# Row normalising and products with inverse sums given to GpSimd as well, in a two-layer attention and MLP kernel ordered by a planner

## The chip, the cores and the metric

The kernel runs on one core of one Trainium2 chip. The metric is device time in microseconds; the kernel before takes 855.15 us (median of 3 runs, 855.11 to 855.25). Five engines of the core work side by side, each through its own instructions in order: TensorE (PE in the profile), VectorE (DVE), ScalarE (ACT), GpSimd (POOL) and SyncE (SP, which issues the DMAs). They wait for each other by semaphores.

## The reference, cut

```python
def _layernorm(x, axis=-1, eps=1e-5):
    m = jnp.mean(x, axis=axis, keepdims=True)
    v = jnp.var(x, axis=axis, keepdims=True)
    return (x - m) / jnp.sqrt(v + eps)
...
    def _A_ref(x, wqkv, wo):                 # x: 1 x 2048 x 448, 16 heads of 28
        qkv = (x @ wqkv).reshape(B, S, 3, H, Dh).transpose(2, 0, 3, 1, 4)
        q, k, v = qkv[0], qkv[1], qkv[2]
        scores = jnp.einsum("bhqd,bhkd->bhqk", q, k) * Dh ** -0.5
        p = _softmax(scores, axis=-1)
        o = jnp.einsum("bhqk,bhkd->bhqd", p, v)
        return o.transpose(0, 2, 1, 3).reshape(B, S, D) @ wo
    def _B_ref(x, w1, b1, w2, b2):           # 448 -> 1792 -> 448
        h = jnp.einsum("bsd,df->bsf", x, w1) + b1
        r = jnp.where(h > 0, h, 0)
        return jnp.einsum("bsf,fd->bsd", r * r, w2) + b2

    x = A_x
    x = x + _A_ref(_layernorm(x), A_wqkv, A_wo)
    x = x + _B_ref(_layernorm(x), B_w1, B_b1, B_w2, B_b2)
    x = x + _A_ref(_layernorm(x), A_wqkv, A_wo)
    x = x + _B_ref(_layernorm(x), B_w1, B_b1, B_w2, B_b2)
    return x
```

## The kernel before

**The work.** Each of the two layers is an attention (A) and an MLP (B), with the same weights. Everything stays in the core's memory; `x_sb` holds the 2048 rows as 16 tiles of 128. Queries are worked on in blocks of 256 (two tiles; the last two of layer 2 are single tiles). The softmax numerators are the bulk: the scores of one head, 128 keys by 256 queries twice, make a *unit* of 128 x 512, and there are 2048 units in all.

**Groups of three.** `s_stream` (matmuls L892) writes three units into one score tile `sc` of 128 x 1536; there are two such tiles. `e_stream` (L917) turns them into `pt` by one exponential on ScalarE. 683 groups make up the run. `p_stream` (L1080) multiplies `pt` with `V_sb` on TensorE into `oT`, whose row 28 of each head holds the sum of the numerators.

**Units on DVE.** Where `apart` returns a unit, the third unit of a group is computed elsewhere and the exponential of that group has 1024 columns. Such a unit takes four steps: on DVE L973 (`take`: scores from PSUM into integers `v_i` or, for the third set of buffers, part of `K_sb`), on DVE L999 (`square`: a polynomial of the fraction, into `v_e`), on GpSimd L995 (`beside`: the power of two from the integer part) and on DVE L1017 (`close`: both multiplied into bf16, into `pt` or a tile of its own). `a_unit` issues the first, `a_rest` the others. `apart` refuses a unit if fewer than `STOP` units are left or fewer than `LEAD` groups have been made, if no set of buffers (two or three) is free, if keys or queries aren't there yet, if the planned load of DVE in the last `SPAN` us is over `BUSY` (`LOW` where the layers' work is behind its due line, `behind`, with `L0E` and `L0N` for layer 1), or if DVE's planned backlog with what such units still owe (`left`) is over `TB`.

**The other work** runs between: layer norms (`layernorm`: statistics L469 and L474 on DVE, variance and inverse root L496 and L497 on GpSimd, normalisation L579 on DVE into `xn`, transpose L519 on PE, copy L531 on DVE), Q, K and V (L634, L638, L666), and per query block a `chain`: output projection, residual L1216, layer norm, MLP with ReLU L1276 and square L1283, residual, and for layer 1 the norm and Q, K, V of layer 2. The first three blocks of layer 1 are `early`.

**Inverse sums.** For most query blocks `norm_pair` takes the sums of two groups of four heads out by DMA (`dn`), inverts them on DVE (L1188), spreads them over all rows by a way through DRAM (`scr`, `rec`), and multiplies `oT_sb` with `rec` into `oTn` (`mul`, L1207, 28 times). The last blocks use `norm_turn`, which does it by transposes on DVE (L1149 to L1165).

**The planner.** The order on each engine is made when the program is built. Every operation is an `Op` with engine, planned duration, operations it depends on and buffers it takes and frees. `Planner.run` picks the operation that can start first, and among equals the stream of the lowest priority number; `earliest` gives start and engine. An `Op` with `port=True` isn't planned on DVE while one is planned on GpSimd, and the other way round; on the chip nothing enforces it. In `earliest` before, the engine is the one that could start first:

```python
        if o.port:
            t = max(t, self.port["POOL" if o.eng[0] == "DVE" else "DVE"])
        ...
            if best is None or s < best[0] - 0.05:
                best = (s, e)
```

Before, L995 has `port=True` and 0.85 us (`EDUR`); L999, L1017, L1207 and L1283 have it on DVE; L579 hasn't. Priorities named in the change: `C_PRIO` for L973, `EPRIO` for L995, `V_WAIT` the time after which the rest of a unit becomes urgent. `NEAR` and `FAR` say how close to the next `p_stream` start a small or large matmul tile may still take a PSUM bank (`spare`); `KEEP` how long `p_stream` may wait for a unit from DVE.

**Filler.** TensorE also does matmuls whose result isn't used: `s_stream` repeats the score matmuls up to `MORE` times where the planned load is under `HOT` and there is room, and `heat` (L1334, `ident` by `xn`) adds one or two where the load is under `HEAT`.

Of the kernel before, what the change touches and what calls it, by code (L numbers as in the profile page):

```python
# [11 lines left out]
DT = mybir.dt  # L12
# [16 lines left out]
EXP_BASE = 91.0 * 2.0 ** 23 + 13573.0 * 2.0 ** 7  # L29
EXP_POLY = (4.803267716767392 * 2.0 ** 16, 14.031064225079138 * 2.0 ** 32)  # L30
OVER = 0.08
EDUR = 0.85
EPRIO = 1.5
EPOOL = 1
EMOD = 1
QUICK = 2
QUICK3 = 2
PRE = 0.5
# [4 lines left out]
DCLK = 0.2  # L43
OWN = 2
HALF = 320
L0E = 1310
L0N = 7.0
L1E = 1900
L1N = 5.6
# [12 lines left out]
AHEAD = (range(0, 4), range(0, 4), range(0, 4), range(0, 1))  # L62
SLACK = 0.5
WINDOW = 2.8
C_PRIO = 3.2
V_PRIO = 8.5
V_LATE = 4.0
V_LAST = 3
# [2 lines left out]
OWN3 = 0  # L71
FIRST = 50
V_FIRST = 9
V_WAIT = 3.5
NEAR = 4
FAR = 17
KEEP = 5
LAG = 12
LEAD = 20
LAST = 690  # L80
BUSY = 0.995
TB = 2.2
TB2 = 0.9
SPAN = 11
NPT = 11
NOS = 2
AEND = 0
HOT = 0.9
MORE = 3
HEAT = 0.76  # L90
HWIN = 3.4
NEAR_U = 0
LASTP = 3.2
# [4 lines left out]
THIRD = 1  # L98
NL = 0
NLP = 4.9  # L100
STOP = 100
HSTOP = 0
CHUNK = 2
EV = 2.9
# [24 lines left out]


class Op:
    __slots__ = ("eng", "dur", "fn", "deps", "acq", "rel", "mode", "sets", "start", "end", "res", "turn", "ready", "lat", "need", "got", "more", "room", "port")

    def __init__(self, eng, dur, fn, deps=(), acq=None, rel=None, mode="full", sets=(), lat=0.0, need=1, port=False):
        self.eng = eng if isinstance(eng, tuple) else (eng,)
        self.dur, self.fn, self.deps, self.mode, self.lat = dur, fn, deps, mode, lat
        self.rel = rel if isinstance(rel, list) else ([] if rel is None else [rel])
        self.acq = acq if isinstance(acq, tuple) or callable(acq) else (() if acq is None else (acq,))
        self.sets = sets if isinstance(sets, list) else ([sets] if sets else [])
        self.start = self.end = self.res = self.turn = None  # L140
        self.need, self.got, self.more, self.port = need, [], 0.0, port
# [5 lines left out]
class Planner:  # L147
# [22 lines left out]
    def earliest(self, o):  # L170
        t = 0.0
        for d in o.deps:
            if not isinstance(d, Op):
                d = self.tok.get(d)
            if d is None or d.end is None:
                return None, None
            same = d.eng[0] == o.eng[0] and len(o.eng) == 1
            t = max(t, d.end + d.lat + ((0.03 if same else 0.10) if d.eng[0] == "DVE" else
                                (0.0 if same and d.eng[0] != "DMA" else LAT[d.eng[0]])))
        acq = o.acq() if callable(o.acq) else o.acq  # L180
        if o.acq:
            free = [r.when() for r in acq if r.when() is not None]
            if not free:
                return None, None
            t = max(t, min(free))
        if o.port:
            t = max(t, self.port["POOL" if o.eng[0] == "DVE" else "DVE"])
        o.ready = t
        best = None
        for e in o.eng:  # L190
            s = max(t, self.clock[e])
            if e == "PE" and self.mode != o.mode:
                s = max(t, self.clock[e] + 0.1)
            if best is None or s < best[0] - 0.05:
                best = (s, e)
        return best

    def run(self):
        while self.streams:
            cands = []  # L200
            for st in self.streams:
                s, e = self.earliest(st[2]) if st[2] is not None else (None, None)
                if s is not None:
                    cands.append((s, st[0](s) if callable(st[0]) else st[0], e, st))
            assert cands, "no stream can go on"
            known = cands

            due = next((c[3][2].ready for c in cands if c[1] == 0), None)
            if due is None:
                due = next((c[0] + c[3][2].dur + LAT["ACT"] for c in cands if c[1] == 1), None)  # L210
            if due is not None:
                ok = [c for c in cands if c[2] != "PE" or c[1] == 0 or c[0] + c[3][2].dur <= due + self.slack()]
                cands = ok or cands
            s, _, e, st = min(cands, key=lambda c: (max(c[3][2].ready, self.clock[c[2]]) if c[2] == "PE" and self.turns() else c[0], c[1]))
            o = st[2]
            o.eng = (e,)
            if o.acq:
# [12 lines left out]
            if e == "PE":  # L230
                self.mode = o.mode
            if e in self.past:
                self.past[e] = [p for p in self.past[e] if p[1] > s - 40.0] + [(s, max(s, self.clock[e]))]
            for a in o.rel:
                a.got.append(o.end + o.lat + LAT[e])
                if len(a.got) == a.need:
                    a.res.rel[a.turn] = max(a.got)
            for key in o.sets:
                self.tok[key] = o
            st[2] = next(st[1], None)  # L240
            if st[2] is None:
                self.streams.remove(st)
# [3 lines left out]
def kernel(  # L246
# [12 lines left out]
    nc = tc.nc  # L259
# [220 lines left out]
    def layernorm(t0, nt, deps_of, early=False, mv=None, place=None, x_in=None, parts=False):  # L480
# [89 lines left out]
        for p0 in range(0, nt, wide):  # L570
            js = range(p0, min(p0 + wide, nt))
            own = Op("DVE", 0.0, None, acq=R_xn)
            yield own
            xs = []
            for j in js:
                xn = xns[2 * (own.turn % 2) + j % 2]

                def norm(e, j=j, xn=xn):
                    nc.vector.tensor_scalar(out=xn[:, 0:D], in0=x_sb[:, t0 + j, :],  # L579
                                            scalar1=mv[0][:, j, 0:1], scalar2=ln[j],  # L580
                                            op0=ALU.subtract, op1=ALU.mult)
                nm = Op("DVE", 0.39, norm, deps=[rss[j], *([] if x_in is None else [x_in])], sets=[("n", t0, j)] if early else ())
                yield nm
                xs.append((xn, nm))

            todo.append((p0, own, xs))
            if early and p0 + wide < nt:
                continue
            while todo:
                p0, own, xs = todo.pop(0)  # L590
                yield from turn(p0, own, xs)
# [370 lines left out]
    def a_unit(gi, x, src, unit, l):  # L962
# [20 lines left out]
    def a_rest(gi, c, box, unit):  # L983

        lin, low = EXP_POLY

        aside = unit[0] % EMOD < EPOOL

        def power(e):
            nc.vector.tensor_scalar(out=box["e"], in0=box["n"], scalar1=2.0 ** 22, scalar2=EXP_BASE,  # L990
                                    op0=ALU.mult, op1=ALU.add)

        def beside(e):
            box["h"], box["e"] = box["e"].bitcast(DT.float32), box["i"]
            nc.gpsimd.tensor_scalar(out=box["e"], in0=box["n"], scalar1=2.0 ** 22, scalar2=EXP_BASE,  # L995
                                    op0=ALU.mult, op1=ALU.add)

        def square(e):
            nc.vector.scalar_tensor_tensor(out=box["e"].bitcast(DT.float32) if aside else box["h"], in0=box["f"], scalar=lin, in1=box["f"],  # L999
                                           op0=ALU.add, op1=ALU.mult)  # L1000
        if aside:
            h = Op("DVE", 0.684, square, deps=[c], port=True)
            yield h
            left[0] -= 0.6
            p = Op("POOL", EDUR, beside, deps=[h], port=True)
            pl.spawn(EPRIO, iter([p]))
        else:
            p = Op("DVE", 0.42, power, deps=[c], port=True)
            yield p
            left[0] -= 0.34  # L1010
            h = Op("DVE", 0.684, square, deps=[c, p], port=True)
            yield h
            left[0] -= 0.6

        def close(e):
            pd = gbuf[gi]["pd"] = gbuf[gi]["pt"][:, 1024:1536] if gbuf[gi]["in"] else pd_of(o)
# [154 lines left out]
    def norm_pair(l, qb, g, pair):  # L1171
# [32 lines left out]
        yield r  # L1204

        def mul(e):
            nc.vector.tensor_tensor(out=oTn_of[l, qb][0][:, g:g + 2, 0:n], in0=both,  # L1207
                                    in1=box["r"][:, :, 0:n], op=ALU.mult)
# [176 lines left out]
```

## Time and profile before

The profiled execution took 857.11 us with its profile; its span, from the first instruction to the last, is 855.3 us. Of that, by engine:

| | busy us | share | what most of it is |
|---|---|---|---|
| PE | 813.1 | 95% | scores 306.9, `oT` from `pt` 153.0; ends of matmuls are modelled |
| ACT | 833.2 | 97% | exponentials L917, 821.4 |
| DVE | 780.0 | 91% | 231 units of three steps |
| POOL | 206.3 | 24% | L995, 164.4 |

A row of the groups reads: line, engine, operation, tile written and read, shapes, number, then busy time and mean duration of one in ns, then idle time before it and what ended it. A row of the timeline reads: start, duration, engine, line, operation, number. A row of the windows gives a stretch, its length, and for PE, weight loads, DVE, ACT and POOL the busy time and the number of instructions, then the granted clock of TensorE. A row of the waits gives who waited for whom, the sum, how often, and the longest.

The exponentials run from 12.3 to 840.6 us. POOL waits for L999 before L995 for 359.8 us in 122 times, which is time in which it has nothing to do.

### The profile page before, as it was taken

To read this page: it belongs to the slowest core of one execution; us is meant where nothing else is said; L and a number is where in the kernel's file an instruction comes from. 1 tells how busy PE (TensorE), PEld (TensorE's weight loads), DVE (VectorE), ACT (ScalarE), POOL (GpSimd) and SP (SyncE) were. 2 spreads that over 40 slices of the span, in tenths; PEclk is the share of its full clock that TensorE was granted. 3 is DMA by queue.
4 is the path that set the end of the run, shared out by engine and by line. 5 is a ranking of instruction groups with operands and counts; after the bars stand their busy time and mean duration, and the time that the engine had idled before them with its cause. 6 is when DMAs were issued, how large, how long until landed. Compare 5 with 4: busy or idle time off the path is not lost.

```text
span 855.3 us, 28520 instructions
## 1 busy us (share of the span) xinstructions
PE 813.1 (95%) x12287; PEld 434.4 (51%) x12287; DVE 780.0 (91%) x1510; ACT 833.2 (97%) x701; POOL 206.3 (24%) x326
## 2 busy tenths in 40 slices
PE   8999999999999999999999999999999999999998
PEld 4555555454545545455445544445544544545656
DVE  7999999999999999999898999999999999989744
ACT  7999999999999999999999999999999999999995
POOL 3211222222222222322222222321222123222100
PEclk9999999999999999999999999999999999999999
DMA  9200100000000000000000000011100000000000
GB/s 248 66 3 2 27 17 15 15 16 15 15 2 15 16 15 14 3 15 14 2 3 2 2 2 2 16 28 28 31 9 20 21 26 26 13 15 15 20 8 19
DMA packets 32315, 17.98 MB, mean 21 GB/s; under 512 B 17786, under 2 KB 31739, under 8 KB 32188
## 3 DMA queue, kind: packets, MB, share of 16 engines
q1 hardware_dynamic: 32188, 16.16, 6.9%
q8 instruction: 96, 1.57, 0.8%
q14 instruction: 31, 0.25, 0.1%
HBM read 13.87 MB, written 2.06 MB: 19 GB/s over the span
## 4 chain that ended last, share of the span: by engine, by line
ACT 41%; PE 32%; DVE 15%; issue 10%; DMA 1%; POOL 1%; ACTq 0%; SPq 0%; DVEq 0%
ACT pt L917 41%; PE mt L615 14%; PE sc L892 11%; PE oT L1080 5%; DVE v_i L973 2%; DVE v_e L999 2%; DVE pt L1017 1%; DVE r L1276 1%; DVE st L469 1%; DVE x_sb L1216 1%; PE sc L615 1%; PE mt L1334 1%; DVE xn L579 1%; DVE K_sb L999 1%; DVE K_sb L973 1%
## 5 line engine op out<-in xcount | busy, mean ns | idle before, releaser
L917 ACT ACTIVATE pt<-sc 128x1536 bf16<-128x1536 f32 (+1 forms) x683 | 821.4, 1403 | 7.6 <-PE sc L892 6.9
L892 PE MATMUL sc<-Q_sb,K_sb 32*128 32x256 bf16 (+1 forms) x5300 | 306.9, 266 | 29.7 <-ACT pt L917 22.2
L892 PEld LDWEIGHTS <-K_sb 32*128 32x128 bf16 x5300 | 135.3, 92 | 206.3 <-issue 155.6
L995 POOL TENSOR_SCALAR v_i<-v_i 128x512 int32<-128x512 int16 x166 | 118.1, 712 | 375.2 <-DVE v_e L999 359.8
L1080 PE MATMUL oT<-pt,V_sb 128*32 128x256 bf16 (+1 forms) x4056 | 153.0, 268 | 0.9 <-ACT pt L917 0.3
L615 PE MATMUL mt<-xnT,w 128*128 128x256 bf16 (+1 forms) x904 | 121.4, 270 | 0.4 <-DVE oTn L1165 0.2
L973 DVE TENSOR_SCALAR v_i<-sc 128x512 int32<-128x512 f32 x166 | 112.8, 680 | 8.0 <-PE sc L892 6.9
L1080 PEld LDWEIGHTS <-V_sb 128*32 128x32 bf16 x4352 | 90.9, 96 | 48.5 <-issue 45.3
L999 DVE SCALAR_TENSOR_TENSOR v_e<-v_i 128x512 f32<-128x512 uint16 x166 | 111.9, 681 | 0.3
L615 PEld LDWEIGHTS <-w 128*128 128x128 bf16 x952 | 77.1, 98 | 37.5 <-issue 29.5
L1276 DVE TENSOR_SCALAR r<-mt 128x512 bf16<-128x512 f32 x108 | 73.3, 679 | 8.4 <-PE mt L615 7.9
L995 POOL TENSOR_SCALAR K_sb<-K_sb 128x512 int32<-128x512 int16 x65 | 46.3, 712 | 141.0 <-DVE K_sb L999 130.4
L615 PE MATMUL mt<-w,V_sb 128*128 128x448 bf16 x274 | 67.6, 355 | 0.0
L1334 PE MATMUL mt<-xn,ident 128*128 128x448 bf16 x151 | 50.9, 356 | 1.4 <-DVE x_sb L1216 0.5
L1216 DVE TENSOR_TENSOR x_sb<-x_sb,mt 128x448 bf16<-128x448 bf16 x61 | 37.2, 610 | 14.4 <-PE mt L615 14.2
L973 DVE TENSOR_SCALAR K_sb<-sc 128x512 int32<-128x512 f32 x65 | 44.2, 681 | 4.6 <-PE sc L892 4.0
L999 DVE SCALAR_TENSOR_TENSOR K_sb<-K_sb 128x512 f32<-128x512 uint16 x65 | 45.0, 693 | 0.2
L1017 DVE SCALAR_TENSOR_TENSOR pt<-v_e,v_i 128x512 bf16<-128x512 f32 x62 | 42.0, 681 | 1.5 <-POOL v_i L995 1.5
L1017 DVE SCALAR_TENSOR_TENSOR V_sb<-v_e,v_i 128x512 bf16<-128x512 f32 x60 | 41.5, 694 | 1.9 <-POOL v_i L995 1.7
L496 POOL TENSOR_TENSOR ve<-mv,eps_t 128x2 f32<-128x2 f32 (+1 forms) x34 | 10.8, 318 | 118.1 <-DVE mv L474 117.9
L469 DVE BATCH_NORM_STATS2 st<-x_sb 128x6 f32<-128x448 bf16 x62 | 38.1, 615 | 0.9 <-DMA x_sb<-in_A_x_dram 0.7
L615 PEld LDWEIGHTS <-V_sb 128*128 128x128 bf16 x302 | 24.7, 98 | 25.0 <-issue 10.7
(105 smaller groups left out, 752.4 us busy)
## 6 DMA issues: line engine op xcount, KB each, us to landing
rec<-scr SPq DMA_DIRECT2D x54, 128.0 KB
x_sb<-in_A_x_dram SPq DMA_DIRECT2D x8, 224.0 KB
out_dram<-x_sb SPq DMA_DIRECT2D x15, 112.0 KB
w<-in_B_w_dram SPq DMA_DIRECT2D x1, 1568.0 KB
w<-in_B_w_dram SPq DMA_DIRECT2D x1, 1344.0 KB
dn<-oT_sb SPq DMA_DIRECT2D x54, 4.0 KB
V_sb<-in_A_wqkv_dram SPq DMA_DIRECT2D x4, 168.0 KB
scr<-dn SPq DMA_DIRECT2D x27, 8.0 KB
```

The source lines that it names most:

```text
L469: nc.vector.bn_stats(out=box["st"][:, :], in_=x_sb[:, t0 + j, :] if src is None else src())
L615: nc.tensor.matmul(box["t"][:, c0:c0 + n], lhsT=lhsT() if callable(lhsT) else lhsT, rhs=rhs, start=a, stop=b)
L892: nc.tensor.matmul(dst[k][:, i * nt * P:(i + 1) * nt * P], lhsT=K_sb[l][rows, g, (kb + i) * P:(kb + i + 1) * P], rhs=Q_sb[rows, g, t0 * P: ...
L917: t = nc.scalar.activation(out=pt[:, 0:n], in_=gbuf[gi]["sc"][:, 0:n], func=AF.Exp, scale=float(np.log(2.0)) * 2.0 ** -FRAC)
L973: t = nc.vector.tensor_scalar(out=box["i"], in0=two(src), scalar1=EXP_BIAS, scalar2=EXP_LOW, op0=ALU.add, op1=ALU.max)
L995: nc.gpsimd.tensor_scalar(out=box["e"], in0=box["n"], scalar1=2.0 ** 22, scalar2=EXP_BASE, op0=ALU.mult, op1=ALU.add)
L999: nc.vector.scalar_tensor_tensor(out=box["e"].bitcast(DT.float32) if aside else box["h"], in0=box["f"], scalar=lin, in1=box["f"], op0=ALU. ...
L1017: nc.vector.scalar_tensor_tensor(out=box["two"](pd), in0=box["h"], scalar=low, in1=box["e"].bitcast(DT.float32), op0=ALU.add, op1=ALU.mult)
L1080: nc.tensor.matmul(box["t"][DHP * hh:DHP * hh + DHP, 0:n], lhsT=V_sb[l][:, kb + i, 4 * g + hh, :], rhs=p[:, c0:c0 + n], start=begin and kb ...
L1216: nc.vector.tensor_tensor(out=x_sb[:, tb, lo:hi], in0=x_sb[:, tb, lo:hi], in1=t[:, 0:hi - lo], op=ALU.add)
L1276: nc.vector.tensor_scalar(out=r[:, 0:w], in0=t[:, 0:w], scalar1=0.0, scalar2=None, op0=ALU.max)
L1334: nc.tensor.matmul(t[:, 0:D], lhsT=ident[:, :], rhs=xns[0][:, 0:D], start=True, stop=True)
```

## The change

1. An operation may name several engines with a duration for each (`durs`). `earliest` now takes the engine on which it would end first, with `ASIDE` (2 us) added to DVE where GpSimd is the other.
2. The normalisation L579 may run on GpSimd (planned 0.6 us) or DVE (0.39), except in the `early` blocks, and has `port=True`. The product L1207 likewise (1.3 on GpSimd).
3. The power of L995 may run on either engine (`EDUR` 0.66 on GpSimd, 0.42 on DVE); a branch that put it on DVE for chosen units, which wasn't in use, is gone. Its order after the square stays.
4. Fourteen planning constants have new values.

```diff
-EDUR = 0.85
-EPRIO = 1.5
-EPOOL = 1
-EMOD = 1
+EDUR = 0.66
+EPRIO = 2.5
+ASIDE = 2.0
+XNP = 1
+XDUR = 0.6
+MULP = 1
+MDUR = 1.3
...
-L0E = 1310
+L0E = 1280
...
-C_PRIO = 3.2
+C_PRIO = 1.6
...
-V_WAIT = 3.5
-NEAR = 4
-FAR = 17
-KEEP = 5
+V_WAIT = 5
+NEAR = 6
+FAR = 9
+KEEP = 6
 LAG = 12
-LEAD = 20
+LEAD = 15
 LAST = 690
-BUSY = 0.995
+BUSY = 0.97
...
-SPAN = 11
+SPAN = 15
...
-MORE = 3
-HEAT = 0.76
+MORE = 1
+HEAT = 0.7
...
-STOP = 100
+STOP = 80
...
-        self.dur, self.fn, self.deps, self.mode, self.lat = dur, fn, deps, mode, lat
+        self.durs = dur if isinstance(dur, tuple) else (dur,) * len(self.eng)
+        self.dur, self.fn, self.deps, self.mode, self.lat = self.durs[0], fn, deps, mode, lat
...
-        if o.port:
-            t = max(t, self.port["POOL" if o.eng[0] == "DVE" else "DVE"])
         o.ready = t
         best = None
-        for e in o.eng:
+        for e, dur in zip(o.eng, o.durs):
             s = max(t, self.clock[e])
             if e == "PE" and self.mode != o.mode:
                 s = max(t, self.clock[e] + 0.1)
-            if best is None or s < best[0] - 0.05:
-                best = (s, e)
-        return best
+            if o.port:
+                s = max(s, self.port["POOL" if e == "DVE" else "DVE"])
+            late = s + (dur + ASIDE * (e == "DVE") if "POOL" in o.eng else 0.0)
+            if best is None or late < best[2] - 0.05:
+                best = (s, e, late)
+        return best[:2]
...
+            o.dur = o.durs[o.eng.index(e)]
             o.eng = (e,)
...
-                    nc.vector.tensor_scalar(out=xn[:, 0:D], in0=x_sb[:, t0 + j, :],
+                    (nc.vector if e == "DVE" else nc.gpsimd).tensor_scalar(out=xn[:, 0:D], in0=x_sb[:, t0 + j, :],
...
-                nm = Op("DVE", 0.39, norm, deps=[rss[j], *([] if x_in is None else [x_in])], sets=[("n", t0, j)] if early else ())
+                nm = Op(*((("POOL", "DVE"), (XDUR, 0.39)) if XNP and not early else ("DVE", 0.39)), norm, port=True, deps=[rss[j], *([] if x_in is None else [x_in])],
+                        sets=[("n", t0, j)] if early else ())
...
-        left[0] += 2.14 - 0.34 * (unit[0] % EMOD < EPOOL)
+        left[0] += 1.8
...
+        def square(e):
+            nc.vector.scalar_tensor_tensor(out=box["h"], in0=box["f"], scalar=lin, in1=box["f"],
+                                           op0=ALU.add, op1=ALU.mult)
+        h = Op("DVE", 0.684, square, deps=[c], port=True)
+        yield h
+        left[0] -= 0.6
...
+        def power(e):
+            (nc.vector if e == "DVE" else nc.gpsimd).tensor_scalar(out=box["e"], in0=box["n"], scalar1=2.0 ** 22, scalar2=EXP_BASE,
+                                                                   op0=ALU.mult, op1=ALU.add)
+        p = Op(("POOL", "DVE"), (EDUR, 0.42), power, deps=[h], port=True)
+        pl.spawn(EPRIO, iter([p]))
...
-            nc.vector.tensor_tensor(out=oTn_of[l, qb][0][:, g:g + 2, 0:n], in0=both,
-                                    in1=box["r"][:, :, 0:n], op=ALU.mult)
-        m = Op("DVE", 0.13 + 2 * n / 930, mul, deps=[r, oTn_of[l, qb][1]], rel=pair["own"], port=True)
+            (nc.vector if e == "DVE" else nc.gpsimd).tensor_tensor(out=oTn_of[l, qb][0][:, g:g + 2, 0:n], in0=both,
+                                                                   in1=box["r"][:, :, 0:n], op=ALU.mult)
+        m = Op(*((("POOL", "DVE"), (MDUR, 0.13 + 2 * n / 930)) if MULP else ("DVE", 0.13 + 2 * n / 930)), mul, deps=[r, oTn_of[l, qb][1]], rel=pair["own"], port=True)
```

More of the change, by code (lines that the diff above doesn't have):

```diff
@@ L131 @@
 class Op:
-    __slots__ = ("eng", "dur", "fn", "deps", "acq", "rel", "mode", "sets", "start", "end", "res", "turn", "ready", "lat", "need", "got", "more", "room", "port")
+    __slots__ = ("eng", "dur", "fn", "deps", "acq", "rel", "mode", "sets", "start", "end", "res", "turn", "ready", "lat", "need", "got", "more", "room", "port", "durs")
     def __init__(self, eng, dur, fn, deps=(), acq=None, rel=None, mode="full", sets=(), lat=0.0, need=1, port=False):
         self.eng = eng if isinstance(eng, tuple) else (eng,)
-        self.dur, self.fn, self.deps, self.mode, self.lat = dur, fn, deps, mode, lat
+        self.durs = dur if isinstance(dur, tuple) else (dur,) * len(self.eng)
+        self.dur, self.fn, self.deps, self.mode, self.lat = self.durs[0], fn, deps, mode, lat
         self.rel = rel if isinstance(rel, list) else ([] if rel is None else [rel])
@@ L578, in norm @@
                 def norm(e, j=j, xn=xn):
-                    nc.vector.tensor_scalar(out=xn[:, 0:D], in0=x_sb[:, t0 + j, :],
-                                            scalar1=mv[0][:, j, 0:1], scalar2=ln[j],
-                                            op0=ALU.subtract, op1=ALU.mult)
-                nm = Op("DVE", 0.39, norm, deps=[rss[j], *([] if x_in is None else [x_in])], sets=[("n", t0, j)] if early else ())
+                    (nc.vector if e == "DVE" else nc.gpsimd).tensor_scalar(out=xn[:, 0:D], in0=x_sb[:, t0 + j, :],
+                                                                           scalar1=mv[0][:, j, 0:1], scalar2=ln[j],
+                                                                           op0=ALU.subtract, op1=ALU.mult)
+                nm = Op(*((("POOL", "DVE"), (XDUR, 0.39)) if XNP and not early else ("DVE", 0.39)), norm, port=True, deps=[rss[j], *([] if x_in is None else [x_in])],
+                        sets=[("n", t0, j)] if early else ())
                 yield nm
@@ L985, in a_rest @@
         lin, low = EXP_POLY
-        aside = unit[0] % EMOD < EPOOL
-        def power(e):
[L990 to L1013, printed above, removed]
+        box["h"], box["e"] = box["e"].bitcast(DT.float32), box["i"]
+        def square(e):
[4 more added lines that the diff above has]
+        left[0] -= 0.6
+        def power(e):
+            (nc.vector if e == "DVE" else nc.gpsimd).tensor_scalar(out=box["e"], in0=box["n"], scalar1=2.0 ** 22, scalar2=EXP_BASE,
+                                                                   op0=ALU.mult, op1=ALU.add)
+        p = Op(("POOL", "DVE"), (EDUR, 0.42), power, deps=[h], port=True)
+        pl.spawn(EPRIO, iter([p]))
         def close(e):
```

## The prediction

> **What bounds the kernel now.** I read the first part of the page, then the chain, then what ScalarE (ACT) waited for.
>
> ```profile
> PE 813.1 (95%) x12287; PEld 434.4 (51%) x12287; DVE 780.0 (91%) x1510; ACT 833.2 (97%) x701; POOL 206.3 (24%) x326
> ...
> ACT 41%; PE 32%; DVE 15%; issue 10%; DMA 1%; POOL 1%; ACTq 0%; SPq 0%; DVEq 0%
> ```
> ```profile
> ACT pt L917 <- PE sc L892: 6.9, 14, 1.2
> ```
>
> ACT is busy 97% of the span, and its exponentials (L917) waited for scores 6.9 us in all. The trace puts the first exponential at 12.3 us and the end of the last at 840.6; before and behind them lie an opening and an end of about 27 us, which this change hardly touches. So the time is the work that ACT has between 12 and 841 us, and what counts is how many blocks of scores VectorE (DVE) takes off it. The groups by form give what one block is worth.
>
> ```profile
> L917 ACT ACTIVATE pt<-sc 128x1536 bf16<-128x1536 f32 x451 | 647.5, 1549 | 3.1 <-PE sc L892 2.4 <-ACT pt L917 0.5
> L917 ACT ACTIVATE pt<-sc 128x1024 bf16<-128x1024 f32 x232 | 253.0, 1121 | 4.6 <-PE sc L892 4.5
> ```
>
> 683 groups of three blocks; in 231 of them DVE takes the third, and the exponential has 1024 columns in place of 1536. The means differ by 0.428 us (neighbours overlap in time, but from end to end the medians of the trace are 1.343 and 0.917, so 0.426). **One more block on DVE shortens ACT's work by 0.43 us.** What it costs DVE, and what the change takes off DVE:
>
> ```profile
> L973 DVE TENSOR_SCALAR v_i<-sc 128x512 int32<-128x512 f32 x166 | 112.8, 680 | 8.0 <-PE sc L892 6.9
> L999 DVE SCALAR_TENSOR_TENSOR v_e<-v_i 128x512 f32<-128x512 uint16 x166 | 111.9, 681 | 0.3
> L1017 DVE SCALAR_TENSOR_TENSOR pt<-v_e,v_i 128x512 bf16<-128x512 f32 x62 | 42.0, 681 | 1.5 <-POOL v_i L995 1.5
> L579 DVE TENSOR_SCALAR xn<-x_sb,mv,rstd 128x448 bf16<-128x448 bf16 x64 | 30.6, 502 | 4.0 <-POOL rstd L497 4.0
> L1207 DVE TENSOR_TENSOR oTn<-oT_sb,rec 128x512 bf16<-128x512 f32 x27 | 18.3, 677 | 0.8 <-DMA rec<-scr 0.8
> ...
> L995 POOL TENSOR_SCALAR v_i<-v_i 128x512 int32<-128x512 int16 x166 | 118.1, 712 | 375.2 <-DVE v_e L999 359.8
> ```
>
> **What is taken off DVE.** Consecutive DVE instructions overlap: in the timeline below a step of 0.68 us begins at 401.66 and the next at 402.26, so one occupies the queue some 0.08 us less than its duration.
>
> ```profile
> 401.66 0.68 DVE L973 TENSOR_SCALAR v_i<-sc 128x512 int32<-128x512 f32 x1
> 402.26 0.69 DVE L579 TENSOR_SCALAR xn<-x_sb,mv,rstd 128x448 bf16<-128x448 bf16 x2
> ```
> ```profile
> 297.54 1.49 DVE L579 TENSOR_SCALAR xn<-x_sb,mv,rstd 128x448 bf16<-128x448 bf16 x2 [0.86 <-POOL rstd L497]
> ```
> ```profile
> 297.59 1.31 POOL L995 TENSOR_SCALAR v_i<-v_i 128x512 int32<-128x512 int16 x2
> ```
>
> Two normalisations take 0.69 us alone, but 1.49 beside two GpSimd powers: they hold each other up. That is why L579's mean is 0.502 and not 0.39, and L995's 0.712 and not 0.62 (its median).
> - Normalisations: 64, of which 6 (three opening blocks) stay. 30.6 - 6 x 0.39 = 28.3 us, less 58 x 0.08 of overlap: 23.7 us.
> - Products with inverse sums: 27 x 0.677 + 0.415 = 18.7, less 28 x 0.08: 16.5 us. The twelve products of L1165 stay.
> - Powers on DVE: the planner may now place them there, but charges 2 us for it; with GpSimd 24% busy I take none.
>
> Sum: 40.2 us of DVE time freed.
>
> **What it buys.** A block costs DVE 0.680 + 0.681 + 0.681 less 3 x 0.08 = 1.80 us. It also shortens the run by 0.43 us, in which DVE would have worked at the share that the long middle stretch shows:
>
> ```profile
> 100.00:800.00 700.00, 669.88 (x9975) 349.75 (x9970) 660.93 (x1244) 694.40 (x584) 180.15 (x274) 1.00 0.05 15
> ...
> 820.00:840.00 20.00, 18.41 (x473) 11.56 (x468) 6.38 (x18) 20.00 (x16) 0.00 (x0) 1.00 0.05 15
> ```
>
> The columns behind the length are PE, weight loads, DVE, ACT, POOL: DVE is busy 660.9 of 700 us (94%), ACT 99%. So 40.2 / (1.80 + 0.94 x 0.43) = 18.2 blocks.
> - STOP 100 to 80 and LEAD 20 to 15 open 20/3 + 5 = 11.7 more groups to DVE. DVE's steps run from 38.0 to 795.4 us; 19 exponentials start before and 34 after, so 231 of 630 groups, 0.37 each: 4.3 blocks. The last stretch has the room (6.4 of 20 us busy), the opening less: 3 blocks.
> - BUSY 0.97 over 15 us in place of 0.995 over 11: bites only where DVE would have been fuller than 97%, with the middle at 94%. Between 0 and 231 x 2.5% = 6 blocks lost; I take 1.5, because most stretches lie below it.
> - Ports: the planner no longer lets a normalisation or product on GpSimd run beside L999, L1017, L1283 on DVE. Between 0 and 6 blocks lost (next part but one); I take 1.
> - EDUR 0.66 in place of 0.85 agrees better with 0.62; C_PRIO, V_WAIT, NEAR, FAR, KEEP shift order. Each could gain or lose a few waits; ACT's scores waits are 6.9 us, so the gain is at most that, and a loss of the same size is my other bound. I take nothing.
>
> 18.2 + 3 - 1.5 - 1 = 18.7 blocks, x 0.43 = **8.0 us**.
>
> **What GpSimd takes on.** No row shows either operation there. A normalisation has one large input, like L995: 0.62 x 448/512 = 0.54 at the least, 0.99 (L995 held up) at the most; I take 0.57. A product has two inputs: at the least 0.62, at the most twice L995 held up, 2.0; if the inputs are read in turn, 1.24, and the diff charges 1.3: I take 1.27. 58 x 0.57 + 28 x 1.27 = 69 us on an engine with 649 idle. L995 should fall to 0.62-0.66, since its rival on the port is gone. Only one normalisation lies on the closing chain, L579 at 844.64 us (0.40): +0.2 us there. Queued behind a normalisation on GpSimd are powers, for which L1017 waits; behind it on PE, in order, stand its transpose and all scores after. The rival on queues prices that. No DMA is moved. A product keeps its `rec` and `oT_sb` tiles some 0.6 us longer, and SP's DMAs for the next pair wait for them, with the output stores queued behind; there are two of each, and L1207 comes every 10 us or more, so I take nothing (if a store were held, it would be by those 0.6 us).
>
> The Trainium skill (GPSIMD Engine Reference, 4.1 Engine selection) advises VectorE for elementwise work, GpSimd being about twice as slow with two inputs; its 3.1 gives about 2.6 cycles an element at 1.2 GHz, an estimate of 1.1 us and dispatch for a product. By that GpSimd's share changes by 5 us and the sum by nothing, for the engine has room.
>
> **The sum.** Span 855.3 - 8.0 + 0.2 = 847.5. The profiled run took 857.1, 1.8 around the span; the runs shown have a median of 855.15, 0.15 below the span. So **847.3 us**. Forecast band 844 to 850.
>
> **Rivals.**
> 1. *More than that* (13%): the DVE steps lose their hold-ups too (L1017 took 1.03 us at 103.10 beside a power), all 4.3 blocks come, and ACT's waits fall from 6.9 to 4: 25 blocks x 0.43 + 2.9 = 13.6, 841.5. For it: L999 and L1017 beside a power mostly take 0.68, so there is little to win there.
> 2. *The port eats the gain* (8%). L1017 at 103.10:
>
> ```profile
> 103.10 1.03 DVE L1017 SCALAR_TENSOR_TENSOR V_sb<-v_e,v_i 128x512 bf16<-128x512 f32 x1
> ```
>
> A power ran on GpSimd from 102.98, and the step took 0.35 us longer. If every added GpSimd microsecond that falls beside such steps (250 x 1.36 us and L1283's 46 in 847, 46%) were lost to DVE: 69 x 0.46 = 32 of the 40 us, 3.8 + 3 blocks, 2.9 us: 852.2. Against: of 69 L999 that overlap a power the mean is 0.698 against 0.679 for the others, and the plan keeps them apart. The Trainium skill (Advanced Engine Details and Errata, Mode Summary) states that such instructions of the two engines block each other; L579 at 297.54 agrees, those 69 mostly not.
> 3. *The freed time isn't used* (6%): the gates on DVE's load and backlog refuse the blocks. Only the 11.7 groups count, less BUSY's losses: 854.5, no change.
> 4. *Slower: PE waits for GpSimd* (11%). GpSimd works in order. A pair of normalisations there takes 2 x 0.57 against 0.69 (+0.45 us), and if a power stands in front, +0.62. The 29 transposes stand in PE's queue ahead of scores. PE has some 0.33 us of slack before ACT runs dry (it waited for ACT 68 times, 22.2 us). 29 x (1.07 - 0.33) = 21 us lost if all are hit; from 0.28 us for each transpose the 8 us are gone. Two in three hit: 861. For it: PE waited for L579 three times already, 2.0 us, up to 1.2. Against: the planner knows the longer duration, and L496 and L497 in front are on GpSimd anyway.
> 5. *Slower: TensorE's clock drops* (4%). MORE 1 and HEAT 0.7 take away filler: L1334's 151 matmuls and part of L892's repeats. The granted clock was 1.00 in every stretch from 20 us on. A slice at half clock lasted 3.4 us and would cost ACT about 1 us; one slice in twelve: +20, 867. Against: the longest gap between matmuls behind 20 us was 1.0 us.
>
> **Chances.** The forecast 58%. Faster by over 0.2% (1.7 us, about what a measurement here can tell from none): 58 + 13 + 8 = 79%; within: 6%; slower: 15%. The range that leaves out a fifth: 840.5 (below it lie ends of rival 1) to 858 (beyond it most of 4 and 5).
>
> **What would show it.** L917 with 1024 columns: about 250 of 683, ACT busy about 825; L579 on POOL x58 near 0.57, L1207 on POOL x28 near 1.27; L995 near 0.64; DVE still 90 to 92% busy. Wrong, if the count of 1024 stays near 231 (rival 3), if L999 and L1017 lengthen to 0.75 or more (2), if ACT's waits for L892 pass 12 us, with PE waiting for POOL (4), or if the clock shows slices below 1 (5).

## The result, and the profile after

The changed kernel takes 913.09 us (median of 4 runs, 910.37 to 914.63) beside 855.2 for the kernel before: ratio 1.067, 95% interval 1.064 to 1.070. The profiled execution took 910.37 us, its span is 908.1. Lines of the changed file are shifted by a few: L585 is the normalisation (L579 before), L1004 the power (L995), L924 the exponential (L917), L1201 the product (L1207), L525 the transpose (L519).

The first part of the page and its clock row, then the chain, of the changed kernel:

```profile
PE 824.1 (91%) x11998; PEld 427.8 (47%) x11998; DVE 764.5 (84%) x1441; ACT 836.4 (92%) x699; POOL 370.4 (41%) x417
...
PEclk9999989999999999999979999999999999989899
...
PE 38%; ACT 19%; DVE 19%; POOL 15%; issue 7%; DMA 0%; POOLq 0%; ACTq 0%; DVEq 0%
ACT pt L924 19%; PE mt L622 17%; PE sc L899 12%; POOL xn L585 11%; PE oT L1074 6%; DVE v_i L980 2%; DVE v_e L997 2%; DVE pt L1011 2%; DVE st L475 2%; PE mt L1328 2%; DVE x_sb L1210 2%; DVE r L1270 2%; POOL rstd L503 2%; POOL v_i L1004 1%; PE tp L525 1%
```

ACT fell from 97% of the span to 92% though its work grew by 3 us only: it stands still. GpSimd went from 206 to 370 us where 275 were forecast, and one of its lines, the normalisation, is now 11% of the chain. The clock row has slices below 9, which the one of before had not:

```profile
PEclk9999999999999999999999999999999999999999
```

The groups by form of the changed kernel (line, engine, operation, tiles, number, busy, mean ns, idle before):

```profile
L585 POOL TENSOR_SCALAR xn<-x_sb,mv,rstd 128x448 bf16<-128x448 bf16 x58 | 123.4, 2133 | 3.9 <-PE tp L525 0.7
L1004 POOL TENSOR_SCALAR v_i<-v_i 128x512 int32<-128x512 int16 x169 | 118.2, 699 | 278.5 <-DVE v_e L997 268.2 <-DVE oT_sb L1100 3.1 <-DVE mv L480 2.2
L1201 POOL TENSOR_TENSOR oTn<-oT_sb,rec 128x512 bf16<-128x512 f32 x27 | 36.7, 1359 | 15.0 <-DMA rec<-scr 13.8 <-PE sc L899 0.2
...
L924 ACT ACTIVATE pt<-sc 128x1536 bf16<-128x1536 f32 x446 | 638.1, 1518 | 35.2 <-PE sc L899 34.2 <-ACT pt L924 0.5
L924 ACT ACTIVATE pt<-sc 128x1024 bf16<-128x1024 f32 x237 | 252.8, 1095 | 21.5 <-PE sc L899 20.7 <-ACT pt L924 0.3
```

A normalisation takes **2.13 us** on GpSimd. The planner was told 0.6; on DVE it took 0.50. The product takes 1.36 where 1.3 was planned. And 237 of the exponentials have 1024 columns where it was 232: **five blocks more**, not nineteen. (One of them is the last group, which has only two blocks, so 236 come from DVE, and 231 before.) The waits of the changed kernel (who for whom, sum, how often, longest):

```profile
ACT pt L924 <- PE sc L899: 54.9, 50, 3.8
...
PEld L525 <- POOL xn L585: 42.5, 34, 2.4
PE tp L525 <- POOL xn L585: 35.2, 29, 2.3
```

ACT's wait for scores went from 6.9 to 54.9 us. The 48 us between them are nearly all of the 52.8 us by which the span grew. One such place in the timeline of the changed kernel, GpSimd, then TensorE, then ScalarE:

```profile
119.84 1.59 POOL L1201 TENSOR_TENSOR oTn<-oT_sb,rec 128x512 bf16<-128x512 f32 x1
121.42 4.07 POOL L585 TENSOR_SCALAR xn<-x_sb,mv,rstd 128x448 bf16<-128x448 bf16 x2
```
```profile
123.34 0.40 PE L525 MATMUL tp<-ident,xn 128*128 128x128 bf16 x4 [0.39 <-POOL xn L585]
125.54 0.61 PE L525 MATMUL tp<-ident,xn 128*128 128x128 bf16 x4 [1.81 <-POOL xn L585]
```
```profile
127.60 1.02 ACT L924 ACTIVATE pt<-sc 128x1024 bf16<-128x1024 f32 x1 [2.85 <-PE sc L899]
```

Two row tiles keep GpSimd for 4.07 us. PE has its transposes queued ahead of the next scores and stands 1.81 us before the second; ACT runs out and stands 2.85. Two windows around it, of the changed kernel (busy of PE, weight loads, DVE, ACT, POOL; then the clock, and the DMA's share and GB/s):

```profile
122.00:125.50 3.50, 0.91 (x11) 0.43 (x10) 1.75 (x3) 2.76 (x3) 3.49 (x2) 1.00 0.01 1
125.50:128.90 3.40, 3.36 (x27) 1.45 (x28) 2.05 (x5) 1.02 (x1) 0.62 (x1) 0.50 0.00 0
```

PE worked 0.91 of 3.5 us, and in the slice behind it the clock is half. The clock records show 13 such stretches between 20 us and the closing of the run, 61 us together; before, none.

### The profile page after: what moved, and what is told of

Same layout as the page of the kernel before. It is cut to its first block, busy times and chain, and to the rows that moved or that the text cites. A ratio compares the mean times of both kernels' runs of the same rounds, so it can differ in the third digit from the quotient of the medians.

```text
span 908.1 us, 28046 instructions
## 1 busy us (share of the span) xinstructions
PE 824.1 (91%) x11998; PEld 427.8 (47%) x11998; DVE 764.5 (84%) x1441; ACT 836.4 (92%) x699; POOL 370.4 (41%) x417
## 4 chain that ended last, share of the span: by engine, by line
PE 38%; ACT 19%; DVE 19%; POOL 15%; issue 7%; DMA 0%; POOLq 0%; ACTq 0%; DVEq 0%
ACT pt L924 19%; PE mt L622 17%; PE sc L899 12%; POOL xn L585 11%; PE oT L1074 6%; DVE v_i L980 2%; DVE v_e L997 2%; DVE pt L1011 2%; DVE st L475 2%; PE mt L1328 2%; DVE x_sb L1210 2%; DVE r L1270 2%; POOL rstd L503 2%; POOL v_i L1004 1%; PE tp L525 1%
## 5 line engine op out<-in xcount | busy, mean ns | idle before, releaser
L924 ACT ACTIVATE pt<-sc 128x1536 bf16<-128x1536 f32 (+1 forms) x683 | 825.5, 1371 | 56.7 <-PE sc L899 54.9
L1004 POOL TENSOR_SCALAR v_i<-v_i 128x512 int32<-128x512 int16 x169 | 118.2, 699 | 278.5 <-DVE v_e L997 268.2
L899 PEld LDWEIGHTS <-K_sb 32*128 32x128 bf16 x5058 | 127.7, 93 | 220.2 <-issue 171.8
L1074 PE MATMUL oT<-pt,V_sb 128*32 128x256 bf16 (+1 forms) x4058 | 156.3, 272 | 1.1 <-DVE pt L1011 0.7
L980 DVE TENSOR_SCALAR v_i<-sc 128x512 int32<-128x512 f32 x169 | 115.6, 685 | 21.2 <-PE sc L899 20.5
L585 POOL TENSOR_SCALAR xn<-x_sb,mv,rstd 128x448 bf16<-128x448 bf16 x58 | 123.4, 2133 | 3.9 <-PE tp L525 0.7
L997 DVE SCALAR_TENSOR_TENSOR v_e<-v_i 128x512 f32<-128x512 uint16 x169 | 116.3, 695 | 0.4
L1004 POOL TENSOR_SCALAR K_sb<-K_sb 128x512 int32<-128x512 int16 x67 | 48.2, 719 | 136.8 <-DVE K_sb L997 119.2
L525 PE MATMUL tp<-ident,xn 128*128 128x128 bf16 x252 | 24.4, 228 | 36.1 <-POOL xn L585 35.2
L1011 DVE SCALAR_TENSOR_TENSOR pt<-v_e,v_i 128x512 bf16<-128x512 f32 x69 | 47.1, 685 | 3.8 <-POOL v_i L1004 3.8
L1201 POOL TENSOR_TENSOR oTn<-oT_sb,rec 128x512 bf16<-128x512 f32 (+1 forms) x28 | 37.4, 1336 | 21.4 <-DMA rec<-scr 20.2
L1328 PE MATMUL mt<-xn,ident 128*128 128x448 bf16 x104 | 38.5, 392 | 6.1 <-POOL xn L585 6.0
```

What stands on the lines that cost most here:

```text
L585: (nc.vector if e == "DVE" else nc.gpsimd).tensor_scalar(out=xn[:, 0:D], in0=x_sb[:, t0 + j, :], scalar1=mv[0][:, j, 0:1], scalar2=ln[j], ...
L899: nc.tensor.matmul(dst[k][:, i * nt * P:(i + 1) * nt * P], lhsT=K_sb[l][rows, g, (kb + i) * P:(kb + i + 1) * P], rhs=Q_sb[rows, g, t0 * P: ...
L924: t = nc.scalar.activation(out=pt[:, 0:n], in_=gbuf[gi]["sc"][:, 0:n], func=AF.Exp, scale=float(np.log(2.0)) * 2.0 ** -FRAC)
L980: t = nc.vector.tensor_scalar(out=box["i"], in0=two(src), scalar1=EXP_BIAS, scalar2=EXP_LOW, op0=ALU.add, op1=ALU.max)
L997: nc.vector.scalar_tensor_tensor(out=box["h"], in0=box["f"], scalar=lin, in1=box["f"], op0=ALU.add, op1=ALU.mult)
L1004: (nc.vector if e == "DVE" else nc.gpsimd).tensor_scalar(out=box["e"], in0=box["n"], scalar1=2.0 ** 22, scalar2=EXP_BASE, op0=ALU.mult, op ...
```

## The experiments

All but the two measurements of forms were timed beside the kernel before, whose median was 855.3 to 855.6. In each diff the minus line is the changed kernel (or the kernel before, where said).

**e1: normalisations back on DVE.**

```diff
-XNP = 1
+XNP = 0
```

> The changed kernel with the 58 normalisations back on DVE (XNP 0); products, powers and all constants as changed. Theory D (a normalisation takes 2.13 us on GpSimd instead of the 0.57 assumed, so transposes in PE's queue wait, ACT runs dry and the clock falls behind that): nearly all of the 58 us comes back, 850 to 860 us, granted clock 0.99 or more, ACT waits for scores under 15 us. Rival F (the smaller filler, MORE 1 and HEAT 0.7, lets the clock fall by itself): the clock stays near 0.97 and the time above 885. Rival M (products on GpSimd): time above 885, with PE waiting for L1201.

860.45 us (ratio 1.005, 1.004 to 1.007), clock 0.998, ACT's wait for scores 10.3 us. As theory D has it; rivals F and M fall as causes of the loss: filler and products are as changed here, and 53 of the 58 us are gone.

```profile
ACT pt L924 <- PE sc L899: 10.3, 10, 3.2
```

**e2: filler as before.**

```diff
-MORE = 1
-HEAT = 0.7
+MORE = 3
+HEAT = 0.76
```

> The changed kernel with MORE 3 and HEAT 0.76 as before; normalisations stay on GpSimd. Theory D: the waits for the normalisation stay (PE on xn 60 us or more in all), the filler can't be issued while PE's queue stands still, so the clock stays below 0.98 and the time above 895. Rival F: clock 0.99 or more and the time below 880.

916.99 us (ratio 1.073, 1.070 to 1.076), clock 0.968. More filler doesn't hold the clock while PE's queue stands: theory D.

**e3: the kernel before with the normalisations on GpSimd, nothing else.**

```diff
-                    nc.vector.tensor_scalar(out=xn[:, 0:D], in0=x_sb[:, t0 + j, :],
+                    (nc.gpsimd if e == "POOL" else nc.vector).tensor_scalar(out=xn[:, 0:D], in0=x_sb[:, t0 + j, :],
...
-                nm = Op("DVE", 0.39, norm, deps=[rss[j], *([] if x_in is None else [x_in])], sets=[("n", t0, j)] if early else ())
+                nm = Op("DVE" if early else "POOL", 0.39 if early else 0.6, norm, port=not early, deps=[rss[j], *([] if x_in is None else [x_in])], sets=[("n", t0, j)] if early else ())
```

> The kernel before with one edit: the 58 normalisations on GpSimd, planned at 0.6 us; constants, filler, products as before. Theory D: it takes most of the loss by itself, 895 to 925 us, with the normalisation at about 2.1 us on GpSimd and the clock below 0.98. Rivals F and M: no filler or product has changed, so 845 to 865.

920.55 us (ratio 1.074, 1.070 to 1.078), clock 0.975 in the profiled execution. This single edit makes the whole loss: 65 us here, 58 with the other changes.

```profile
L579 POOL TENSOR_SCALAR xn<-x_sb,mv,rstd 128x448 bf16<-128x448 bf16 x58 | 124.2, 2145 | 6.8 <-PE mt L1334 3.1 <-PE tp L519 0.5
```

**e4 and e5: what GpSimd takes for which form.** Behind the last row tile of the kernel before, three instructions of each form, alone on the core.

```diff
+    for k in range(3):
+        nc.gpsimd.tensor_scalar(out=xns[0][:, 0:D], in0=x_sb[:, NTB - 1, :], scalar1=rs[:, 0:1], scalar2=rs[:, 1:2], op0=ALU.subtract, op1=ALU.mult)
+    for k in range(3):
+        nc.gpsimd.tensor_scalar(out=xns[1][:, 0:D], in0=x_sb[:, NTB - 1, :], scalar1=0.5, scalar2=0.25, op0=ALU.subtract, op1=ALU.mult)
...
```

> The kernel before with 18 instructions added on GpSimd behind its last row tile, three of each form, alone on the core (its time means nothing): 128x448 bf16 to bf16 with two per-row scalars, with two constants, with one per-row scalar; 128x448 to f32 with two per-row scalars; to bf16 with one per-row scalar and one constant; 128x224 to f32 with two per-row scalars. Theory P (the per-row scalars make it slow): about 1.87 us with two, 0.55 with two constants, between them with one. Rival B (bf16 in or out makes it slow): 1.87 with constants too, and less with f32 out. Rival H (held up by DVE in the kernel): all about 0.57 when alone.

Groups of e4: L1359 two per-row scalars, L1365 the same to f32, L1361 two constants, L1363 a multiplication alone, L1369 half the columns:

```profile
L1359 POOL TENSOR_SCALAR xn<-x_sb,mhalf 128x448 bf16<-128x448 bf16 x3 | 5.6, 1860 | 8.5 <-DVE x_sb L1216 8.3
L1365 POOL TENSOR_SCALAR v_e<-x_sb,mhalf 128x448 f32<-128x448 bf16 x3 | 5.6, 1858 | 0.2
...
L1361 POOL TENSOR_SCALAR xn<-x_sb 128x448 bf16<-128x448 bf16 x3 | 5.1, 1708 | 0.2
L1363 POOL TENSOR_SCALAR xn<-x_sb,mhalf 128x448 bf16<-128x448 bf16 x3 | 4.2, 1403 | 0.2
L1369 POOL TENSOR_SCALAR v_e<-x_sb,mhalf 128x224 f32<-128x224 bf16 x3 | 3.3, 1108 | 0.2
```

None of the three theories: it is slow alone (against H), slow with constants (against P), and with f32 out it takes 1.86 too (against B, as far as the output goes). Between it and the power at 0.62 stood the types and the pair of operations. So e5 crossed them.

> As e4, 18 instructions behind the last row tile on GpSimd, three of each (its time means nothing). e4 had subtract-then-multiply slow (1.71 us) even with two constants, while the kernel's power (multiply-then-add with constants, 128x512 int16 to int32) takes 0.62. Theory O (the pair of operations decides): multiply-then-add takes 0.55 to 0.65 on 128x448 bf16, with constants and with two per-row scalars; subtract-then-multiply and add-then-multiply take 1.7 us or more, on int16 to int32 too. Rival T (the types decide: bf16 is slow, int16 is not): multiply-then-add on bf16 takes about 1.7 too, and subtract-then-multiply on int16 to int32 about 0.6.

Groups of e5: L1362 and L1366 subtract then multiply; L1358, L1360, L1364 multiply then add; L1368 add then multiply; constants in L1360, L1364 and L1366:

```profile
L1362 POOL TENSOR_SCALAR xn<-x_sb,mhalf 128x448 bf16<-128x448 bf16 x3 | 5.6, 1860 | 0.2
L1366 POOL TENSOR_SCALAR v_e<-v_i 128x448 int32<-128x448 int16 x3 | 5.1, 1709 | 0.2
L1358 POOL TENSOR_SCALAR xn<-x_sb,mhalf 128x448 bf16<-128x448 bf16 x3 | 2.1, 715 | 8.5 <-DVE x_sb L1216 8.3
L1368 POOL TENSOR_SCALAR xn<-x_sb,mhalf 128x448 bf16<-128x448 bf16 x3 | 2.1, 713 | 0.3
L1364 POOL TENSOR_SCALAR v_e<-v_i 128x448 int32<-128x448 int16 x3 | 1.7, 565 | 0.2
L1360 POOL TENSOR_SCALAR xn<-x_sb 128x448 bf16<-128x448 bf16 x3 | 1.7, 564 | 0.2
```

**The pair of operations decides**, not the types: multiply-then-add is 0.56 with constants on either type, subtract-then-multiply 1.71 on either. Per-row scalars add 0.15. Theory O was wrong in one point: add-then-multiply is fast as well (0.71), so in a pair it is the subtraction in front that is slow. That is not the whole rule: e4's multiplication alone, with no subtraction, took 1.40. What the fast forms have in common was not tried further.

**e6: the planner is told the true duration.**

```diff
-XDUR = 0.6
+XDUR = 1.9
```

> The changed kernel with one number: the planner is told 1.9 us for a normalisation on GpSimd instead of 0.6. It still stays there. Theory Q (most of the 58 us comes from the wrong number: PE's queue has the transposes, and all behind them, before the rows are ready): PE's waits for the normalisation fall below 15 us, the clock is back at 0.99 or more, 865 to 880 us. Rival L (the slow instruction itself costs it, through GpSimd's queue and the port it shares): above 895 us with the clock below 0.98.

874.09 us (ratio 1.020, 1.018 to 1.023), clock 0.992. Waits for the normalisation in e6:

```profile
ACT pt L924 <- PE sc L899: 16.2, 19, 2.5
...
PE mt L1328 <- POOL xn L585: 5.2, 4, 1.5
...
PEld L525 <- POOL xn L585: 0.9, 4, 0.3
```

The instruction is as slow as before (1.99 us), but PE finds its rows ready. So 39 us of the loss came from the order that the wrong number made, though the units on DVE fell to 222 (from 236).

**e9: the normalisation as add-then-multiply.** GpSimd makes the negative means behind the inverse roots, 0.29 us for two tiles.

```diff
-XDUR = 0.6
+XDUR = 0.72
...
                 nc.gpsimd.tensor_tensor(out=rstd[:, a:b], in0=ve[:, a:b], in1=mhalf[:, a:b], op=ALU.pow)
+                if not early:
+                    nc.gpsimd.tensor_scalar(out=rstd[:, a + 2:b + 2], in0=mv[0][:, a:b, 0], scalar1=-1.0, scalar2=None, op0=ALU.mult)
+                    for j in range(a, b):
+                        negs[j] = rstd[:, j + 2:j + 3]
-            rs = Op("POOL", 0.95, rsqrt, deps=[mv[1][b - 1]], sets=[("rs", t0 + a)] if early else ())
+            rs = Op("POOL", 0.95 if early else 1.2, rsqrt, deps=[mv[1][b - 1]], sets=[("rs", t0 + a)] if early else ())
...
-                                                                           scalar1=mv[0][:, j, 0:1], scalar2=ln[j],
-                                                                           op0=ALU.subtract, op1=ALU.mult)
+                                                                           scalar1=negs[j], scalar2=ln[j],
+                                                                           op0=ALU.add, op1=ALU.mult)
```

> The changed kernel with the normalisation written as add-then-multiply: GpSimd also makes the negative mean of two row tiles (one small instruction behind the inverse root), and a normalisation there is (x + negative mean) x inverse root, which e5 measured at 0.71 us; the planner is told 0.72, and 1.2 in place of 0.95 for the inverse root. Products stay on GpSimd, constants as changed. Theory O (the operation pair was the trouble): normalisation 0.7 to 0.8 us, clock 0.99 or more, 855 to 864 us, and no faster than before, since e1, e7 and e8 show that the products on GpSimd cost 5 to 7 us and freed DVE time hardly becomes blocks. Rival L (normalising rows on GpSimd costs the time through its queue, whatever the duration): 875 or more.

863.34 us (ratio 1.009, 1.008 to 1.011), clock 0.996. In e9:

```profile
L593 POOL TENSOR_SCALAR xn<-x_sb,rstd 128x448 bf16<-128x448 bf16 x58 | 50.8, 881 | 3.5 <-POOL rstd L505 0.2
```

0.88 us in the kernel, somewhat over the 0.7 to 0.8 expected, and 50 us of the loss are gone. This run changes the instruction and the number together; by e6 the number alone is worth 39 of the 50. Rival L falls. But it is still slower than before, with DVE at 753 us instead of 780: the freed time is idle.

**e7: products on DVE too.**

```diff
-XNP = 1
+XNP = 0
...
-MULP = 1
+MULP = 0
```

> The changed kernel with normalisations and products on DVE: what is left is the constants and the planner's choice for the power. e1 (normalisations on DVE, products on GpSimd) took 860.4. If the products on GpSimd are the cause of e1's 5 us over before: 853 to 856. If the constants are: 859 to 862.

856.07 us (ratio 1.000, 0.999 to 1.001). The constants and the free choice for the power together neither gain nor lose (no power went to DVE); the products on GpSimd cost the 4.4 us between e7 and e1. All five blocks came with them: DVE takes 231 in e7, 236 in e1, and 236 again where the normalisations move too.

**e8: the kernel before with the products on GpSimd, nothing else.**

```diff
-            nc.vector.tensor_tensor(out=oTn_of[l, qb][0][:, g:g + 2, 0:n], in0=both,
+            nc.gpsimd.tensor_tensor(out=oTn_of[l, qb][0][:, g:g + 2, 0:n], in0=both,
...
-        m = Op("DVE", 0.13 + 2 * n / 930, mul, deps=[r, oTn_of[l, qb][1]], rel=pair["own"], port=True)
+        m = Op("POOL", 1.3, mul, deps=[r, oTn_of[l, qb][1]], rel=pair["own"], port=True)
```

> The kernel before with one edit: the 28 products on GpSimd, planned at 1.3 us (measured 1.34). By the prediction's sum for this part (16.5 us of DVE freed, 7.5 blocks of scores): 3 us faster, 852. If, as the changed kernel's count of blocks says (236 against 231), freed DVE time hardly becomes blocks: within 2 us of before, or slower by up to 4.

862.01 us (ratio 1.007, 1.006 to 1.009): 6.5 us slower, more than either theory had. The blocks on DVE are 231, as before. A place of its timeline, DVE and GpSimd:

```profile
676.90 1.80 DVE L1017 SCALAR_TENSOR_TENSOR pd<-v_e,v_i 128x512 bf16<-128x512 f32 x1
```
```profile
676.88 1.26 POOL L1207 TENSOR_TENSOR oTn<-oT_sb,rec 128x512 bf16<-128x512 f32 x1
```

The step of 0.68 us began 0.02 us behind the product and took until 0.56 us after its end. Eight DVE steps of this kernel took 1.4 to 1.8 us so. A step that reads PSUM is not held: L973 at 312.53 us began 0.15 us behind a product and took 0.69. L999, L1017 and L1283 together took 11 us more than before, and ACT's wait for scores rose by 4.4 us. That the one makes the other is not shown, and one thing speaks against it: the plan, in which no step is held up, is already as much longer. When the program is built, the last planned operation ends at 861.3 us in e8 and at 854.4 in the kernel before. So the loss lies in the planned order already.

**e10 and e11: a pace chosen for the durations that were measured.** Constants were drawn anew and chosen by the end of the plan. e10 has normalisations and products on DVE:

```diff
-XNP = 1
+XNP = 0
...
-MULP = 1
+MULP = 0
...
-L0E = 1280
+L0E = 1310
...
-V_WAIT = 5
-NEAR = 6
+V_WAIT = 2.5
+NEAR = 4
...
-KEEP = 6
+KEEP = 5
...
-LEAD = 15
+LEAD = 20
...
-BUSY = 0.97
-TB = 2.2
+BUSY = 0.995
+TB = 1.9
```

> A version meant to beat both: the changed kernel with normalisations and products on DVE, the power left to the planner, and a pace chosen anew for the durations that the chip showed (ASIDE 2, V_WAIT 2.5, NEAR 4, KEEP 5, LEAD 20, L0E 1310, BUSY 0.995, TB 1.9). Theory: GpSimd has nothing to give here but the power, and only the order is left to win: 848 to 853. Rival: orders are worth nothing that the chip keeps: 854 to 858, as e7.

**848.81 us** (ratio 0.992, 0.991 to 0.993): faster than both kernels, within the theory's 848 to 853, and its plan ends at 848.4. Which of the constants does it was not tried. In e10 ACT waits 2.5 us for scores, 235 exponentials have 1024 columns, and the last one ends at 830.7 us (before: 840.6):

```profile
PE 794.7 (94%) x12064; PEld 425.7 (50%) x12064; DVE 781.2 (92%) x1521; ACT 829.1 (98%) x699; POOL 209.8 (25%) x329
```

e11 has the normalisations on DVE in the form of e9, 19 products on GpSimd, and another draw of constants:

```diff
-ASIDE = 2.0
-XNP = 1
+ASIDE = 0.5
+XNP = 0
...
-V_WAIT = 5
+V_WAIT = 2.5
...
-KEEP = 6
+KEEP = 5
...
-LEAD = 15
+LEAD = 20
...
-BUSY = 0.97
-TB = 2.2
+BUSY = 0.995
+TB = 1.9
...
-STOP = 80
+STOP = 100
```

> The other version: normalisations on DVE (as add-then-multiply, with GpSimd's negative means), products on GpSimd only where the planner's penalty for DVE of 0.5 us lets them (19 of 28), pace chosen anew (ASIDE 0.5, V_WAIT 2.5, KEEP 5, LEAD 20, BUSY 0.995, STOP 100, TB 1.9). If products on GpSimd cost by holding up DVE's two-input steps (e8), 19 of them still cost some 4 us: 851 to 858, and slower than the version with all on DVE. If e8's loss came from the pace alone: 847 to 851.

850.38 us (ratio 0.994, 0.993 to 0.996): slower than e10, but in the range for a loss that comes from the pace, and just below the one for products that hold DVE up. The draw differs as well, so the price of its 19 products stays open.

## Why the prediction was wrong

**What bounds the kernel** held: ACT, with 0.43 us for a block. So time in which ACT stands is paid, and its waits for scores grew by 48 us.

**"A normalisation has one large input, like L995: 0.62 x 448/512 = 0.54 at the least, 0.99 at the most; I take 0.57"** is the step that failed. It took 2.13, beyond the upper bound (also beyond 1.30, the longest L995 of that trace, which the bound should have been). The row I called nearest has the same engine and nearly the same shape but another pair of operations (multiply, add), and e5 shows that the pair makes the factor of three. The row's name in the profile, TENSOR_SCALAR, doesn't tell pairs apart; the code does. The planner's 0.6 is off by as much, and so the forecast and the plan agreed: when built, the changed kernel's plan ends at 846.2 us, near the 847.3 of the sum, though with five blocks more and not nineteen. That agreement was luck.

**Rival 4 (PE waits for GpSimd)** had the mechanism: transposes in PE's queue ahead of scores. It was priced with a pair at 1.14 us instead of 4.07, so 861 instead of 913. With the measured pair its own sum would be 29 x (4.07 - 0.69 - 0.33) = 88 us if all are hit, without a power in front. The other half of its argument, that the planner knows the duration, was wrong just because it did not; e6 shows it to be right once it does.

**Rival 5 (the clock)** saw the clock fall for another reason. I looked for it in less filler (e1: clock 0.998 with that filler); it fell behind PE's waits. How much of the 50 us is waiting and how much the 61 us at half clock is not separated.

**"18.2 + 3 - 1.5 - 1 = 18.7 blocks"** failed by itself: 5 came, 2 us. The blocks are fixed when the program is built, so it is the planned DVE time that counts. In e8 16.5 us of it were freed and not one block came; in e9, with DVE busy 753 us in place of 780, there was one more. So freed DVE time alone doesn't bring blocks. What holds them back is not settled. When the program is built, `apart` refuses a unit 451 times before and 446 times after; a missing free set of buffers is 260 and 278 of these, the backlog `TB` 86 and 89, the load `BUSY` 30 and 19. But `apart` asks for the sets first, and in 190 of the 260 the backlog was over `TB` as well. The other candidate is the term that I took as one block, the planner's port rule: what goes to GpSimd keeps L999, L1017 and L1283 out of DVE's plan for as long. With 0.6, 0.72 and 1.9 us planned for a normalisation there, DVE takes 236, 232 and 222 blocks (changed kernel, e9, e6). And e8 planned without that rule for the product has 237 blocks where it had 231; this is a plan alone, which ends at 856.2 us and was not run. A plan is one draw of the order, so this doesn't prove it; if it is the price, the term was nearer 6 than 1 for the product.

**The port.** I took one block for it and gave the rival that it eats the gain 8%. For the normalisation it mattered little: in e3, 38 of L999 and L1017 began while one ran, and took 0.71 us on average. For the product, e8 loses 6.5 us and e7 gets 4.4 back, but by the two plans of e8 (861.3 and 856.2) most of that would lie in keeping the steps apart, not in steps held up on the chip. The observation I set against the port (69 steps at 0.698 us) was an average over steps that overlapped any GpSimd instruction, and most of them had begun before it. In the same trace 12 of L999 began while a power ran: they took 0.80 us on average and up to 1.10, and 11 of them ended 0.5 to 0.6 us after the power did. So the power holds such steps as the product does; it is only shorter.

**The sum as it came out**, from the medians: subtraction first and its wrong number 49.8 us (913.1 to e9's 863.3), normalising on GpSimd even so 2.9 (to e1's 860.4), products 4.4 (to e7's 856.1), the rest 0.6 (to 855.5): 57.6 us. What I took as zero, that the constants only shift order, is right for the changed ones (e7), but order is worth 7 us, as e10 shows.

## What to carry to other kernels

Before an operation is moved to another engine, measure that very operation there, with its pair of operations and its scalars, since a row with the same name and shape can be three times off; a planner that orders queues in advance turns such an error into waits on an engine that had nothing to do with it. Ask what limits the work that is to fill the freed time: here idle DVE time didn't turn into more blocks. Where a planner makes the order, read its plan before the run: the five blocks of the changed kernel and the loss of e8 were both in it. An instruction on GpSimd that holds up DVE steps can cost either way: on the chip, or in a plan that keeps the two apart.

## What the runs showed of the hardware

- GpSimd's tensor-scalar on 128x448, alone (e4, e5): subtract-then-multiply 1.71 us with constants and 1.86 with per-row scalars, a multiplication alone with a per-row scalar 1.40, multiply-then-add 0.56 and 0.71, add-then-multiply 0.71. With 224 columns the slow one takes 1.11, so about 3.3 ns a column ((1.86 - 1.11) / 224) over some 0.36 us.
- TensorE's clock went to half for 3.4 to 10 us after slices of 3.4 us in which PE stood 1.5 to 2.7 us, its longest single gap before them 1.5 to 2.6 us (changed kernel). The Trainium skill (TensorE: Matmul & The Clock Gate, Why this matters for your kernels) advises against gaps over about 3 us; here shorter ones were enough. Not each of them was: two gaps of 1.82 us, at 152.2 and 756.4 us, were split between two slices, at most 1.24 us in either, and the clock stayed full.
- A two-input DVE step that begins while a product runs on GpSimd ends 0.3 to 0.6 us after the product: 0.68 us became 1.80. In e8, 17 of 18 such steps of L999, L1017 and L1283 did. A power holds them too (up to 1.10 in the kernel before); the slow normalisation mostly did not (0.71 on average, e3). Steps that read PSUM kept their 0.68 beside products (L973 and L1276, e8).
